# Attention on one Trainium2 core: score banks in fixed groups, wider exponentials, one bank read by two engines, the output product between the value halves

## The chip, the cores and the metric

The kernel runs on one core of one Trainium2 chip. The metric is the device time of one execution, in microseconds (us). A core has five engines with queues of their own: TensorE (PE; its weight loads are listed apart as PEld), VectorE (DVE), ScalarE (ACT), GpSimd (POOL) and SyncE (SP, which issues transfers). They wait for each other through semaphores. Matrix products land in PSUM, which has eight banks of 512 float32 columns in 128 partitions; PSUM is emptied by ScalarE or VectorE.

## The reference

One sequence of S = 2048 tokens with D = 448 features; `x` goes through two branches, mixed by a gate for each token.

```python
g = sigmoid((x * gate_w).sum(-1, keepdims=True))
# attention: 16 heads of 28 features, one shared key and value head
q = (x @ wq) in 16 heads;  k = x @ wk;  v = x @ wv
a = (softmax(q k^T * 28 ** -0.5) v, heads side by side) @ wo
# mixer: shifted tokens, then an MLP, both after a layernorm
x1 = x + shift(gelu(layernorm(x) @ w1)) @ w2
b = x1 + gelu(layernorm(x1) @ w3) @ w4
out = g * a + (1 - g) * b
```

## The kernel before, in words

The program has three stages: projections and token mixing, the MLP, and from about 395 us on the attention, the only stage that the change touches. The instruction order of every engine is the order in which the code issues them.

The attention works in units. A unit `u` is one block of 512 queries and one group of four heads (4 blocks x 4 groups, `NU` = 16 units). A unit has 16 key tiles of 128 keys, taken two at a time, so it has `NV` = 8 steps `v`; the loop over `k` (L1020) runs through 127 steps, and the last one is written out behind it as the tail (L1056 to L1136). One step does this:

- **Scores** (`scores`, L953): for a key tile, four heads side by side, each into a PSUM bank of its own with keys in the partitions and 512 queries in the columns. Three products a head (high and low parts, L958), the four heads of one product issued together: a *score group*. Two key tiles make six groups.
- **Exponentials** (`exps`, L975): ScalarE reads three of the four banks, 512 columns each, and writes exponentials `p` (L985). The fourth bank, head 3 (`DRAIN`), is copied unchanged to SBUF by VectorE (`pd`, L982). When both key tiles are done, ScalarE takes the exponential of both copies in place, 1024 columns in one instruction (`late_exps`, L990).
- **Output product** (`wo_half`, L881): a quarter-sized piece of the product with `wo` for an earlier unit, four 32-partition strips of 224 columns (L859), added to the output by VectorE (`by_one`, L853). Early steps have a piece of the MLP's last product instead (`w4_job`, `w4_half`); the last unit's steps 4 to 6 have two pieces.
- **Values** (`values`, L1002): for the step before, the exponentials times the values and a column of ones (L995), in two halves of 256 queries (`HALVES`). A half sums both key tiles in one bank; VectorE adds it to the unit's running sum `o` (L999) or, in a unit's first step, copies it (L1010). In the profile the float32 product shows as two instructions, so a half is four *value groups* of four.
- Once a unit, its sums are read back, inverted and multiplied in (`sums_begin`, `recip`, `norm`).

What sets the order around the change: PSUM banks are a list. `take()` takes the bank at its front; whoever issues the instruction that empties a bank puts it back at the end. So which banks a step uses moves on from step to step, and each instruction waits for what used its bank last. Exponentials go to a ring of `PB` = 18 tiles, copies to a ring of `PD` = 3.

Of the kernel before, what the change touches and what calls it, by code (L numbers as in the profile page):

```python
# [31 lines left out]
PB = 18  # L32
# [10 lines left out]
def gated_mix_kernel(  # L43
# [16 lines left out]
    psA = ctx.enter_context(tc.tile_pool(name="psA", bufs=1, space=PSUM))  # L60
# [722 lines left out]


    with tc.tile_pool(name="s3", bufs=1, reuse_waits="tile") as s3, \
# [4 lines left out]
        banks = [mm_tile("bank_0"), mm_tile("bank_1"), misc_tile("bank_2"), max_tile("bank_7")]  # L790
        banks += [ps3.tile([P, 512], F32, name=f"bank_{i}") for i in range(3, 7)]
# [70 lines left out]
        def wo_end(u, t, ps, evict=by_one, queue=nc.sync, cols=slice(0, D)):  # L862
# [4 lines left out]
            banks.append(ps)  # L867
# [5 lines left out]
        def wo_job(u, t, cols=slice(0, D), evict=by_one, queue=nc.sync):  # L873
            b, g = divmod(u, NG)
            ps = take()
# [3 lines left out]
            return wo_end(u, t, ps, evict, queue, cols)  # L879

        def wo_half(u, i):  # L881
            t, h = divmod(i, 2)
            wo_job(u, t, slice(224 * h, 224 * h + 224))

        def w4_job(t):
# [3 lines left out]
            ps = bank(f"job_{n}")[:, 0:D]  # L889
# [5 lines left out]
        def w4_half(k, i):  # L895
# [3 lines left out]
            ps = take()  # L899
# [5 lines left out]
            banks.append(ps)  # L905
# [47 lines left out]
        def scores(u, kt):  # L953
            bs = [take() for j in range(4)]
# [5 lines left out]

        p_free = [s3.tile([P, 512], F32, name=f"p_{i}") for i in range(PB)]
        pd_free = [s3.tile([P, 2, 512], F32, name=f"pd_{i}") for i in range(PD)]
# [12 lines left out]
        def exps(u, kt, bs):  # L975
            ps = p_of[u, kt] = {}
            for j in READ:
                if j == DRAIN:
                    if kt % 2 == 0:
                        pd_of[u, kt // 2] = turn_of(pd_free)  # L980
                    ps[j] = pd_of[u, kt // 2][:, kt % 2, :]
                    nc.vector.tensor_copy(ps[j], bs[j])  # L982
                else:
                    ps[j] = turn_of(p_free)
                    behind[kt % 2] = nc.scalar.activation(ps[j], bs[j], AF.Exp, scale=SCALE)  # L985
                banks.append(bs[j])
# [6 lines left out]
        def value(u, kt, q, pv, start, stop):  # L993
            for j in range(4):
                nc.tensor.matmul(pv[32 * j:32 * j + 32, q], vext[:, kt, :], p_of[u, kt][j][:, q],  # L995
                                 start=start, stop=stop, tile_position=(0, 32 * j))

        def add_value(u, q, pv):
            nc.vector.tensor_add(o_of[u][:, q], o_of[u][:, q], pv[:, q])  # L999
            banks.append(pv)  # L1000

        def values(u, v):  # L1002
            if v == 0:
                o_of[u] = s3.tile([P, 512], F32, tag="o", bufs=2, name=f"o_{u}")
            for q in HALVES:
                pv = take()
                for kt in (2 * v, 2 * v + 1):
                    value(u, kt, q, pv, kt % 2 == 0, kt % 2 == 1)
                if v == 0:
                    nc.vector.tensor_copy(o_of[u][:, q], pv[:, q])  # L1010
                    banks.append(pv)
                else:
                    add_value(u, q, pv)
# [3 lines left out]
        READ = (0, 3, 1, 2)  # L1017
        DRAIN = 3

        for k in range(NU * NV - 1):  # L1020
# [7 lines left out]
            for kt in (2 * v, 2 * v + 1):  # L1028
                exps(u, kt, scores(u, kt))
            late_exps(u, v)  # L1030
            if k == 0:
                for t in range(3):
                    w4_job(t)
            if k in (2, 3):
                w4_half(1, k + 4)
            if 4 <= k < 12:
                w4_half(0, k - 4)
            if k == 11:
                weigh_x1(NT - 4, NT)
            if v >= 4 and u:  # L1040
                wo_half(u - 1, v - 4)
            if v < 4 and u > 1:
                wo_half(u - 2, v + 4)
            if v >= 4 and u == NU - 1:
                wo_half(u - 1, v)
# [35 lines left out]
        p14 = p_of[u, NT - 2] = {j: turn_of(p_free) for j in range(DRAIN)}  # L1081
        p14[DRAIN] = turn_of(pd_free)[:, 0, :]
        p15 = p_of[u, NT - 1] = {j: turn_of(p_free) for j in range(4)}
        nc.vector.tensor_copy(p14[DRAIN], b14[DRAIN])
        nc.scalar.activation(p14[0], b14[0], AF.Exp, scale=SCALE)
        for q in HALVES:
            for p, ps in [(p14[1], b14[1]), (p14[2], b14[2]), (p14[DRAIN], p14[DRAIN])] + [(p15[j], b15[j]) for j in READ]:
# [5 lines left out]
        value(u, NT - 4, q0, pvs[0], True, False)  # L1093
        value(u, NT - 3, q0, pvs[0], False, False)
        value(u, NT - 4, q1, pvs[1], True, False)
        value(u, NT - 2, q0, pvs[0], False, False)
        value(u, NT - 1, q0, pvs[0], False, True)
        banks.extend((b14[1], b14[2]))
        add_value(u, q0, pvs[0])
        value(u, NT - 3, q1, pvs[1], False, False)  # L1100
        value(u, NT - 2, q1, pvs[1], False, False)
# [6 lines left out]
        with tc.block():  # L1108
            tc.mark_branch_hint_location("redo", "LikelyTaken", [mybir.EngineType.PE])
            value(u, NT - 1, q1, pvs[1], False, True)  # L1110
        banks.extend(b15)
        add_value(u, q1, pvs[1])
        tail_back(blocks[1])
# [7 lines left out]
        wo_end(u, 1, joint[1])  # L1121
        nc.sync.dma_start(*store0)
# [11 lines left out]
        wo_end(u, 3, joint[3], by_one, nc.scalar)  # L1134
        again = nc.values_load(redo, min_val=0, max_val=P,
# [61 lines left out]
```

## Time and profile before

| What | us |
|---|---|
| median of 3 runs (lowest to highest) | 908.76 (908.12 to 908.85) |
| the profiled execution's own time | 907.61 |
| its span, first to last instruction | 905.8 |
| busy PE / ACT / DVE / POOL in the span | 899.7 / 632.9 / 543.4 / 105.8 |
| late exponentials (L990): count, first and last start | 127, 398.4 and 890.5 |

Times in the profile count from the span's start. A row of a timeline gives start, duration, engine, line, operation, output and inputs; rows of instructions that follow each other are merged, with the count behind the x. Square brackets hold the idle time ahead of an instruction and the instruction that ended it. Recorded durations of one engine may overlap, so its pace is read from start to start.

### The profile page before, as it was taken

Reading aid. Unit: us, or ns where it says so; the run is one execution under the profiler, and the core shown is the slowest. Engines: PE = TensorE matmul, PEld = TensorE weight load, DVE = VectorE, ACT = ScalarE, POOL = GpSimd, SP = SyncE. Lnnn points to the kernel's source line nnn. Section 1 sums busy time; section 2 is a strip of 40 time slices with the busy share of each in tenths; the row PEclk is TensorE's granted clock in tenths of the full one; section 3 lists DMA queues with packets and bytes.
Section 4 is the critical chain, followed back from the end, with each engine's and each line's share of the span. In section 5 each row is a group of like instructions: output and inputs, shape, how many; then the busy total and the mean of one; then the engine's idle time right before and its main releaser. Section 6 shows DMA issues by size and latency. Waiting matters only on the chain.

```text
span 905.8 us, 24129 instructions
## 1 busy us (share of the span) xinstructions
PE 899.7 (99%) x10097; PEld 644.9 (71%) x10097; DVE 543.4 (60%) x1085; ACT 632.9 (70%) x1135; POOL 105.8 (12%) x138
## 2 busy tenths in 40 slices
PE   9999999999999999999999999999999999999997
PEld 7899888888888888875565655655556556565564
DVE  4655364531435646456666676676667766666665
ACT  5443254332131222269999999999999999999995
POOL 3134100221000520011200000000000000000000
PEclk9999999999999999999999999999999999999999
DMA  8876852310312232120000001000011000010001
GB/s 301 318 169 154 231 177 88 72 40 17 64 48 55 45 87 63 27 65 13 26 27 3 26 26 48 22 26 26 7 43 46 26 3 26 19 53 13 15 14 44
DMA packets 50368, 58.23 MB, mean 64 GB/s; under 512 B 9376, under 2 KB 34768, under 8 KB 50256
## 3 DMA queue, kind: packets, MB, share of 16 engines
q1 hardware_dynamic: 47088, 50.95, 20.1%
q10 hardware_dynamic: 3168, 5.70, 1.8%
q8 instruction: 80, 1.31, 0.6%
q14 instruction: 32, 0.26, 0.1%
HBM read 39.80 MB, written 15.59 MB: 61 GB/s over the span
## 4 chain that ended last, share of the span: by engine, by line
PE 99%; ACT 0%; DVE 0%; issue 0%; ACTq 0%; DVEq 0%
PE bank L995 24%; PE bank L958 23%; PE bank L859 8%; PE acc L709 5%; PE acc L708 5%; PE acc L710 5%; PE g L132 4%; PE g L131 4%; PE g L133 4%; PE hs L477 1%; PE hs L478 1%; PE g L134 1%; PE g L135 1%; PE hs L480 1%; PE h L429 1%; PE h L427 1%
## 5 line engine op out<-in xcount | busy, mean ns | idle before, releaser
L985 ACT ACTIVATE p<-bank 128x512 f32<-128x512 f32 x762 | 386.9, 617 | 2.1 <-PE bank L958 2.0
L995 PE MATMUL bank<-p,vext 128*32 128x256 f32 x3076 | 244.4, 379 | 0.0
L995 PE MATMUL bank<-pd,vext 128*32 128x256 f32 x1020 | 241.1, 379 | 0.0
L982 DVE COPY pd<-bank 128x512 f32<-128x512 f32 x254 | 175.3, 691 | 50.6 <-PE bank L958 49.2
L995 PEld LDWEIGHTS bank<-p,vext 128*32 128x32 f32 x3076 | 126.4, 110 | 82.1 <-ACT p L985 0.5
L697 ACT ACTIVATE gh<-g 128x512 fp32r<-128x512 f32 x54 | 32.2, 597 | 182.0 <-PE g L135 182.0
L999 DVE TENSOR_TENSOR o<-o,bank 128x256 f32<-128x256 f32 x222 | 93.5, 421 | 92.5 <-ACT p L985 54.1
L990 ACT ACTIVATE pd<-pd 128x1024 f32<-128x1024 f32 x127 | 141.0, 1110 | 0.0
L958 PE MATMUL bank<-qh,kH 30*128 30x512 f32 x1024 | 117.9, 444 | 0.0
L995 PEld LDWEIGHTS bank<-pd,vext 128*32 128x32 f32 x1020 | 111.9, 110 | 0.1
L700 DVE TENSOR_TENSOR gl<-gf,gh 128x512 fp32r<-128x512 f32 x54 | 37.2, 688 | 117.7 <-ACT gf L698 117.6
L958 PE MATMUL bank<-qh,kL 28*128 28x512 f32 x1024 | 105.0, 392 | 0.0
L958 PE MATMUL bank<-ql,kH 28*128 28x512 f32 x1024 | 105.0, 391 | 0.0
L958 PEld LDWEIGHTS bank<-qh,kH 30*128 30x128 f32 x1024 | 60.7, 182 | 58.0 <-ACT p L985 46.0
L709 PE MATMUL acc<-w4l,gh 128*128 128x448 f32 x216 | 78.9, 365 | 0.0
L708 PE MATMUL acc<-w4h,gh 128*128 128x448 f32 x216 | 78.8, 365 | 0.0
L710 PE MATMUL acc<-w4h,gl 128*128 128x448 f32 x216 | 78.7, 364 | 0.0
L859 PE MATMUL bank<-wof,on 128*32 128x224 f32 x1008 | 73.1, 367 | 0.0
L132 PE MATMUL g<-al,w3h 128*128 128x512 f32 x168 | 65.8, 392 | 0.0
L131 PE MATMUL g<-ah,w3h 128*128 128x512 f32 x168 | 65.6, 390 | 0.0
L133 PE MATMUL g<-ah,w3l 128*128 128x512 f32 x168 | 65.5, 390 | 0.0
L958 PEld LDWEIGHTS bank<-ql,kH 28*128 28x128 f32 x1024 | 51.6, 185 | 9.2
(203 smaller groups left out, 1158.8 us busy)
## 6 DMA issues: line engine op xcount, KB each, us to landing
qd<-qf ACTq DMA_DIRECT2D x16, 256.0 KB
qm<-qd SPq DMA_DIRECT2D x16, 256.0 KB
qr<-qd SPq DMA_DIRECT2D x16, 256.0 KB
rb<-rd SPq DMA_DIRECT2D x15, 256.0 KB
x<-in_x_dram SPq DMA_DIRECT2D x4, 896.0 KB
hd<-ht SPq DMA_DIRECT2D x16, 224.0 KB
hr<-hd SPq DMA_DIRECT2D x8, 448.0 KB
w34raw<-in_w_dram SPq DMA_DIRECT2D x7, 512.0 KB
```

Of the source, the lines that this page charges most:

```text
L131: nc.tensor.matmul(ps, wh[:, c, :], ah[:, c, :], start=(c == 0), stop=False)
L132: nc.tensor.matmul(ps, wh[:, c, :], al[:, c, :], start=False, stop=False)
L133: nc.tensor.matmul(ps, wl[:, c, :], ah[:, c, :], start=False, stop=False)
L708: nc.tensor.matmul(ps, gh[:, tok], w4h[i][:, k, :], start=(f == 0), stop=False)
L709: nc.tensor.matmul(ps, gh[:, tok], w4l[i][:, k, :], start=False, stop=False)
L710: nc.tensor.matmul(ps, gl[:, tok], w4h[i][:, k, :], start=False, stop=(f == stop))
L859: nc.tensor.matmul(ps[32 * j:32 * j + 32, cols], on_of[u][:, tok], wof[:, u % NG, cols], start=start, stop=stop, tile_position=(0, 32 * j))
L958: nc.tensor.matmul(bs[j], w, a, start=(i == 0), stop=(i == 2), tile_position=(32 * j, 0))
L982: nc.vector.tensor_copy(ps[j], bs[j])
L985: behind[kt % 2] = nc.scalar.activation(ps[j], bs[j], AF.Exp, scale=SCALE)
L990: ins = nc.scalar.activation(pd, pd, AF.Exp, scale=SCALE)
L995: nc.tensor.matmul(pv[32 * j:32 * j + 32, q], vext[:, kt, :], p_of[u, kt][j][:, q], start=start, stop=stop, tile_position=(0, 32 * j))
```

## The change

PSUM in the attention stage is no longer a list of eight single banks. The pool of the earlier stages (`psA`) is closed first, and five fixed tiles are made: for even key tiles `even_0` (one bank), `even_12` (two) and `even_3` (one), for odd key tiles `odd_012` (three) and `odd_3` (one). Scores of head j go to bank j of their group.

ScalarE empties `even_0` and `even_12` with one instruction each (512 and 1024 columns) and `odd_012` with one of 1536. `even_3` is split: VectorE copies columns 256 to 511 and ScalarE takes the exponential of columns 0 to 255. `odd_3` is copied whole by VectorE. The copies, 256 and 512 columns, lie side by side in one tile of 768, and the late exponential covers these. A step so has five exponentials over the same 4096 columns in place of seven.

The value halves have fixed banks: half 0 goes to `even_3`, half 1 to `odd_3` (`single`). `values` is called once for each half; half 0 comes right behind the scores, then the output product (in `even_0`), the sums' check and the norm where due, then half 1. The tail is adapted in names only; it keeps its order. The diff, cut:

```diff
-        banks = [mm_tile("bank_0"), mm_tile("bank_1"), misc_tile("bank_2"), max_tile("bank_7")]
-        banks += [ps3.tile([P, 512], F32, name=f"bank_{i}") for i in range(3, 7)]
+        even = [ps3.tile([P, 512], F32, name="even_0"), ps3.tile([P, 2, 512], F32, name="even_12"),
+                ps3.tile([P, 512], F32, name="even_3")]
+        odd = [ps3.tile([P, 3, 512], F32, name="odd_012"), ps3.tile([P, 512], F32, name="odd_3")]
+        heads = [[even[0], even[1][:, 0, :], even[1][:, 1, :], even[2]],
+                 [odd[0][:, j, :] for j in range(3)] + [odd[1]]]
+        single = [even[2], odd[1]]
+        banks = []
...
         def scores(u, kt):
-            bs = [take() for j in range(4)]
+            bs = heads[kt % 2]
...
-        def exps(u, kt, bs):
-            ps = p_of[u, kt] = {}
-            for j in READ:
-                if j == DRAIN:
-                    if kt % 2 == 0:
-                        pd_of[u, kt // 2] = turn_of(pd_free)
-                    ps[j] = pd_of[u, kt // 2][:, kt % 2, :]
-                    nc.vector.tensor_copy(ps[j], bs[j])
-                else:
-                    ps[j] = turn_of(p_free)
-                    behind[kt % 2] = nc.scalar.activation(ps[j], bs[j], AF.Exp, scale=SCALE)
-                banks.append(bs[j])
+        def exps(u, v):
+            pd = pd_of[u, v] = turn_of(pd_free)
+            pe, po = turn_of(pe_free), turn_of(po_free)
+            scores(u, 2 * v)
+            nc.vector.tensor_copy(pd[:, 0:256], even[2][:, HALVES[1]])
+            nc.scalar.activation(pe[:, 1536:1792], even[2][:, HALVES[0]], AF.Exp, scale=SCALE)
+            nc.scalar.activation(pe[:, 0:512], even[0], AF.Exp, scale=SCALE)
+            behind[0] = nc.scalar.activation(pe[:, 512:1536], even[1].rearrange("p j q -> p (j q)"), AF.Exp, scale=SCALE)
...
+            scores(u, 2 * v + 1)
+            nc.vector.tensor_copy(pd[:, 256:768], odd[1])
+            nc.scalar.activation(po, odd[0], AF.Exp, scale=SCALE)
...
-            for kt in (2 * v, 2 * v + 1):
-                exps(u, kt, scores(u, kt))
+            exps(u, v)
             late_exps(u, v)
...
+            else:
+                values(*divmod(k - 1, NV), 0)
...
             if v >= 4 and u:
-                wo_half(u - 1, v - 4)
+                wo_half(u - 1, v - 4, even[0])
...
-            if k:
-                values(*divmod(k - 1, NV))
-            if u and v == 0:
-                sums.append(sums_begin(u - 1, o_of[u - 1]))
             if u and v == 1:
                 norms.append(recip(*sums.pop()))
             if u and v == 3:
                 norm(*norms.pop())
+            if k:
+                values(*divmod(k - 1, NV), 1)
+            if u and v == 0:
+                sums.append(sums_begin(u - 1, o_of[u - 1]))
```

How the built program stands, at three places. The number behind a tile's name is the build's own; brackets name the semaphores that an instruction waits for, by the engine that raises them. First ScalarE, one step of unit 13, before (banks `bank_*`, exponentials `p_*`, copies `pd_*`):

```order
L985 ACTIVATE p_6_3504<-bank_6_3491 128x512 [waits PE_49]
L985 ACTIVATE p_7_3505<-bank_1_3485 128x512 [waits PE_49]
L985 ACTIVATE p_8_3506<-bank_0_3484 128x512 [waits PE_49]
L985 ACTIVATE p_9_3507<-bank_7_3487 128x512 [waits PE_49]
L985 ACTIVATE p_10_3508<-bank_4_3489 128x512 [waits DVE_49,PE_49]
L985 ACTIVATE p_11_3509<-bank_3_3488 128x512 [waits DVE_49,PE_49]
L990 ACTIVATE pd_1_3517<-pd_1_3517 128x1024 [waits DVE_49,Activation_49]
```

and now (the first row is the late exponential of the step before; `pe_*` and `po_*` hold the exponentials of even and odd key tiles):

```order
L1009 ACTIVATE pd_2_3504<-pd_2_3504 128x768 [waits DVE_49,Activation_49]
L998 ACTIVATE pe_0_3496<-even_3_3487 128x256 [waits DVE_49]
L999 ACTIVATE pe_0_3496<-even_0_3485 128x512
L1000 ACTIVATE pe_0_3496<-even_12_3486 128x1024
L1004 ACTIVATE po_0_3499<-odd_012_3488 128x1536 [waits PE_49]
```

Seven rows became five; the one that reads `even_3` stands first and waits for VectorE, and those of `even_0` and `even_12` behind it have no wait of their own. Then VectorE, one step of unit 13, before:

```order
L982 COPY pd_2_3518<-bank_4_3489 128x512 [waits PE_49]
L982 COPY pd_2_3518<-bank_1_3485 128x512 [waits PE_49]
L853 SCALAR_TENSOR_TENSOR ot_13_9978<-bank_0_3484,gg_75,x1_72 128x224 [waits PE_49,DMAHW7_49,Activation_49,Pool_49]
L999 TENSOR_TENSOR o_13_9683<-o_13_9683,bank_4_3489 128x256 [waits DVE_49,PE_49]
L999 TENSOR_TENSOR o_13_9683<-o_13_9683,bank_7_3487 128x256 [waits DVE_49,PE_49,Activation_49]
```

and now:

```order
L997 COPY pd_1_3503<-even_3_3487 128x256 [waits PE_49]
L1003 COPY pd_1_3503<-odd_3_3489 128x512 [waits PE_49]
L1018 TENSOR_TENSOR o_13_9451<-o_13_9451,even_3_3487 128x256 [waits PE_49,Activation_49]
L859 SCALAR_TENSOR_TENSOR ot_12_9638<-even_0_3485,gg_75,x1_72 128x224 [waits PE_49,Activation_49]
L1018 TENSOR_TENSOR o_13_9451<-o_13_9451,odd_3_3489 128x256 [waits DVE_49,PE_49]
```

The first copy is half as wide, and the output product's eviction (L853, now L859) moved from ahead of both value additions to between them. Last TensorE, from the output product into the values in unit 14, before:

```order
L859 MATMUL bank_2_3486<-wof_3482,on_6_7014 32x224 [waits Activation_49]
L859 MATMUL bank_2_3486<-wof_3482,on_6_7014 32x224 x3
L995 MATMUL bank_6_3491<-p_12_3510,vext_73 32x256 [waits DVE_49]
L995 MATMUL bank_6_3491<-p_13_3511,vext_73 32x256
L995 MATMUL bank_6_3491<-p_14_3512,vext_73 32x256
L995 MATMUL bank_6_3491<-pd_2_3518,vext_73 32x256
```

and now, from the last odd scores to the next even scores:

```order
L966 MATMUL odd_3_3489<-ql_6_5634,kH_1020 128x512
L1014 MATMUL even_3_3487<-pe_2_3498,vext_73 32x256 [waits Activation_49]
L1014 MATMUL even_3_3487<-pe_2_3498,vext_73 32x256 x3
L1014 MATMUL even_3_3487<-po_2_3501,vext_73 32x256 x3
L1014 MATMUL even_3_3487<-pd_2_3504,vext_73 32x256
L865 MATMUL even_0_3485<-wof_3483,on_5_6421 32x224 [waits Activation_49]
L865 MATMUL even_0_3485<-wof_3483,on_5_6421 32x224 x3
L1014 MATMUL odd_3_3489<-pe_2_3498,vext_73 32x256 [waits DVE_49]
L1014 MATMUL odd_3_3489<-pe_2_3498,vext_73 32x256 x2
L1014 MATMUL odd_3_3489<-pd_2_3504,vext_73 32x256
L1014 MATMUL odd_3_3489<-po_2_3501,vext_73 32x256 x3
L1014 MATMUL odd_3_3489<-pd_2_3504,vext_73 32x256
```

The first value half now stands ahead of the product and waits for ScalarE; the product waits for ScalarE's reading of `even_0`, and the second half for VectorE's copy of `odd_3`.

More of the change, by code (lines that the diff above doesn't have):

```diff
@@ L871, in wo_end, with wo_job @@
             return store
-        def wo_job(u, t, cols=slice(0, D), evict=by_one, queue=nc.sync):
+        def wo_job(u, t, cols=slice(0, D), evict=by_one, queue=nc.sync, ps=None):
             b, g = divmod(u, NG)
-            ps = take()
+            own = ps is None
+            if own:
+                ps = take()
             wo_part(u, t, cols, ps, True, True)
@@ L878, in wo_job, with wo_half, w4_job @@
                 ot_of[4 * b + t] = s3.tile([P, D], F32, tag="ot", bufs=5, name=f"ot_{4 * b + t}")
-            return wo_end(u, t, ps, evict, queue, cols)
-        def wo_half(u, i):
+            store = wo_end(u, t, ps, evict, queue, cols)
+            if own:
+                banks.append(ps)
+            return store
+        def wo_half(u, i, ps):
             t, h = divmod(i, 2)
-            wo_job(u, t, slice(224 * h, 224 * h + 224))
-        def w4_job(t):
+            wo_job(u, t, slice(224 * h, 224 * h + 224), ps=ps)
+        def w4_job(t, ps):
             n = NT - 4 + t
@@ L1109, in gated_mix_kernel @@
             tc.mark_branch_hint_location("redo", "LikelyTaken", [mybir.EngineType.PE])
[L1110 removed]
+            value(u, NT - 1, 1, pvs[1], False, True)
         banks.extend(b15)
         add_value(u, q1, pvs[1])
+        banks.append(pvs[1])
         tail_back(blocks[1])
@@ L1121, in gated_mix_kernel @@
         wo_end(u, 1, joint[1])
+        banks.append(joint[1])
         nc.sync.dma_start(*store0)
```

90 lines of the change are left out of this document (49 added, 41 removed).

## The prediction

> **What bounds the kernel now.** The page comes first: the share of each engine, its slices, and the chain that ended last.
>
> ```profile
> span 905.8 us, 24129 instructions
> PE 899.7 (99%) x10097; PEld 644.9 (71%) x10097; DVE 543.4 (60%) x1085; ACT 632.9 (70%) x1135; POOL 105.8 (12%) x138
> ...
> ACT  5443254332131222269999999999999999999995
> ...
> PE 99%; ACT 0%; DVE 0%; issue 0%; ACTq 0%; DVEq 0%
> ```
>
> PE is busy in 99% of the span and carries the chain, but ScalarE (ACT) changes in slice 19: from there on, the attention stage, it is full. The change touches only that stage, so it is read apart. The busy time of 100 us in its middle:
>
> ```profile
> core 0: us, PE busy (x) PEld busy (x) DVE busy (x) ACT busy (x) POOL busy (x), PEclk, DMA share, GB/s
> 500.00:600.00 100.00, 100.00 (x1648) 60.26 (x1648) 69.45 (x139) 100.00 (x181) 5.68 (x6) 1.00 0.11 33
> ```
>
> Both PE and ACT read 100, at full granted clock. Matmuls overlap, so a busy PE may still wait; the timeline of one step, engine by engine (ScalarE, TensorE, its weight loads PEld, VectorE), tells which of the two sets the pace. Rows give start, duration, engine and line, in brackets the idle time ahead and who ended it:
>
> ```profile
> 605.08 1.11 ACT L990 ACTIVATE pd<-pd 128x1024 f32<-128x1024 f32 x1
> 606.10 3.04 ACT L985 ACTIVATE p<-bank 128x512 f32<-128x512 f32 x6
> 608.97 1.11 ACT L990 ACTIVATE pd<-pd 128x1024 f32<-128x1024 f32 x1
> ```
> ```profile
> 605.09 0.51 PE L958 MATMUL bank<-qh,kH 30*128 30x512 f32 x4
> 605.43 0.40 PE L958 MATMUL bank<-qh,kL 28*128 28x512 f32 x4
> 605.66 0.40 PE L958 MATMUL bank<-ql,kH 28*128 28x512 f32 x4
> ...
> 606.75 0.58 PE L859 MATMUL bank<-wof,on 128*32 128x224 f32 x8
> 607.15 0.39 PE L995 MATMUL bank<-p,vext 128*32 128x256 f32 x3
> ...
> 607.80 0.39 PE L995 MATMUL bank<-p,vext 128*32 128x256 f32 x3
> ...
> 608.66 0.39 PE L995 MATMUL bank<-p,vext 128*32 128x256 f32 x3
> ```
> ```profile
> 605.09 0.19 PEld L958 LDWEIGHTS bank<-qh,kH 30*128 30x128 f32 x4 [0.41 <-ACT p L985]
> ...
> 606.75 0.16 PEld L859 LDWEIGHTS bank<-wof,on 128*32 128x32 f32 x8 [0.42 <-ACT p L985]
> ```
> ```profile
> 606.20 1.40 DVE L982 COPY pd<-bank 128x512 f32<-128x512 f32 x2 [0.49 <-PE bank L958]
> 607.51 0.44 DVE L853 SCALAR_TENSOR_TENSOR ot<-bank,gg,ot 128x224 f32<-128x224 f32 x1
> 608.26 0.42 DVE L999 TENSOR_TENSOR o<-o,bank 128x256 f32<-128x256 f32 x1 [0.31 <-PE bank L995]
> ```
>
> A step is 608.97 - 605.08 = 3.89 us, and ACT has no idle time in it: one late exponential (1.02 to the next start) and six of 512 columns, (608.97 - 606.10) / 6 = 0.478 each. PE waits for ACT twice (the brackets on PEld). Its own work is six score groups at 0.23 (605.43 to 605.66), one output product at 0.40 (606.75 to 607.15) and eight value groups at (608.66 - 607.15) / 7 = 0.216, 1.38 + 0.40 + 1.73 = 3.51. So ACT sets the pace, with PE 0.38 behind it.
>
> **The change, part by part.** *Fewer, wider exponentials.* Five replace seven over the same 4096 columns. What one instruction costs beside its columns comes from the tail, where exponentials of 256 columns stand back to back:
>
> ```profile
> 892.67 0.39 ACT L1088 ACTIVATE p<-bank 128x256 f32<-128x256 f32 x1
> ...
> 893.24 1.78 ACT L1088 ACTIVATE p<-bank 128x256 f32<-128x256 f32 x6
> 894.82 0.49 ACT L1088 ACTIVATE pd<-pd 128x256 f32<-128x256 f32 x1
> ```
>
> Six starts take 894.82 - 893.24 = 1.58, 0.263 each; 512 columns took 0.478, so 256 columns are 0.215 and the fixed part is 0.05. The new sum, start to start: 0.26 (256) + 0.48 (512) + 0.91 (1024) + 1.34 (1536) + 0.81 (the late one, 768 columns: 1.02 - 0.215) = 3.79. If ACT kept the pace, a step would gain 0.10. No row reads several banks in one instruction. Its bounds are these sums and, if each further bank were charged like an instruction of its own, 0.15 more, 3.94; I take no extra charge, since a column costs the same in all the rows.
>
> The Trainium skill ("ScalarE: Activation LUTs", What ACT_TABLE_LOAD costs) gives an ACTIVATE without pointer operands 186 ns plus 0.833 ns a column, with back-to-back ones overlapping by about 93 ns. By it seven would cost some 4.06 and five 3.88, a gain of 0.19; the measured step of 3.89 is below 4.06, so the row's 0.05 is used.
>
> *The bank that two engines empty.* In the built order L998, ACT's exponential of 256 columns of even_3, waits for VectorE (DVE) alone, no longer for PE. It can learn that the scores are there only from L997, DVE's copy of the other half of that bank, which itself waits for PE. So the two reads stand one behind the other, DVE first. Behind the waiting L998 in ACT's queue are the exponentials of even_0 and even_12, whose banks are ready at the same time, and everything after them. And PE's first value group writes even_3, so it waits for L998.
>
> *The output product between the values, fixed banks.* Before, each score set, product and value half took the banks that were freed longest ago, and the first value half needed none that the step's last scores had just filled. Now PE runs even scores, odd scores, values half 0 (into even_3), product (even_0), values half 1 (odd_3), even scores. The product's 0.40 is moved, not added. This is a loop through three engines, and its length is added up from the start of the even scores. The copy of 256 columns and the hand-overs have these rows:
>
> ```profile
> L1010 DVE COPY o<-bank x32: 423/425/426, 401.3 to 870.5; 128x256 f32<-128x256 f32 x32
> ```
> ```profile
> 377.87 0.59 ACT L698 ACTIVATE gf<-g 128x512 f32<-128x512 f32 x1
> ```
> ```profile
> 378.49 0.69 DVE L700 TENSOR_TENSOR gl<-gf,gh 128x512 fp32r<-128x512 f32 x1 [1.53 <-ACT gf L698]
> ```
> ```profile
> 896.75 0.31 DVE L1077 STREAM_TRANSPOSE on<-scaled 128x128 f32<-128x128 f32 x1
> ```
> ```profile
> 897.11 0.16 PEld L859 LDWEIGHTS bank<-wof,on 128*32 128x32 f32 x8 [0.50 <-DVE on L1077]
> ```
>
> - even scores, first group to third: 2 x 0.23 = 0.46; third group's start to DVE's copy: 606.20 - 605.66 = 0.54 (even_3 is written last in each group, as the copied bank was);
> - copy of 256 columns: 0.43;
> - DVE to ACT: no row shows ACT waiting for DVE; ACT to DVE took 378.49 - (377.87 + 0.59) = 0.03, DVE to PE 897.11 - (896.75 + 0.31) = 0.05, PE to DVE 606.20 - (605.66 + 0.40) = 0.14. I take 0.05, bounds 0.03 and 0.14;
> - exponential of 256 columns to its end: 0.39 (the row at 892.67);
> - ACT to PE: 0.05 again; PE's restart after idling: 0 to 0.11 (the score group at 605.09 was followed after 0.34 instead of 0.23); the product at 606.75, of the values' kind, took 0.20 a group from a standstill, so I take 0.02;
> - values 4 x 0.216 = 0.87, product 0.40, values 0.86.
>
> Sum: 0.46 + 0.54 + 0.43 + 0.05 + 0.39 + 0.05 + 0.02 + 0.87 + 0.40 + 0.86 = 4.07. Of the 1.94 ahead of the values the odd scores cover PE up to 1.38; 0.56 is idle. ACT's 3.79 fits in with 0.28 to spare, so its gain is hidden by this loop.
>
> Other waits in the loop: odd scores need odd_012 read. ACT starts L998 at 1.48 (0.46 + 0.54 + 0.43 + 0.05) and reaches the odd banks 1.65 later, at 3.13; 1.34 and a hand-over later, at some 4.6, they are free, 0.1 ahead of the next odd scores (4.07 + 0.69). Half 1 needs the copy of odd_3, done by 1.15 (the third odd group) + 0.54 + 0.70 (half of 1.40) = 2.4, ahead of its 3.2. PE's next even scores need even_0 evicted: from the start of half 0, its last group at 0.65, 0.46 to DVE's add (607.80 to 608.26), the add 0.42, the eviction 0.44, 0.05, together 2.02, plus a cold restart of 0.11: 2.13, exactly PE's own 2.13. The loop holds with nothing to spare there. SP's DMAs and POOL's splits keep their order and their steps; the sums' readback (15 units) has its reader moved ahead of values half 1, 0.9 us earlier in a step, and is taken as hidden.
>
> **The sum.** The late exponentials count the steps:
>
> ```profile
> L990 ACT ACTIVATE pd<-pd x127: 1104/1107/1247, 398.4 to 890.5; 128x1024 f32<-128x1024 f32 x127
> ```
> ```profile
> 881.98 1.10 ACT L990 ACTIVATE pd<-pd 128x1024 f32<-128x1024 f32 x1
> 883.37 3.05 ACT L985 ACTIVATE p<-bank 128x512 f32<-128x512 f32 x6 [0.29 <-PE bank L958]
> 886.24 1.11 ACT L990 ACTIVATE pd<-pd 128x1024 f32<-128x1024 f32 x1
> ```
>
> 126 steps take 492.1 us. The first two, without the full set of work, I leave at 3.8 (ACT's sum); the last two hold a second product and took 4.26 with ACT waiting for PE, which shows that PE's loop before was 4.26 - 0.40 = 3.86, just under ACT's 3.89. After: 2 x 3.8 + 122 x 4.07 + 2 x 4.47 = 513.1, 21.0 more. The start and the tail keep their instructions and are left at zero; the tail's score and value groups wait for each other as before, and I allow 1 us either way. The profiled execution took 907.61 us (905.8 of span and 1.8 around it), so 928.6; the median of the runs shown, 908.76, is 1.15 above that execution: 930, rounded.
>
> **The rivals.** *ACT keeps the pace (faster).* If the two reads of even_3 ran side by side, the loop would lose the 0.43 and 0.05 (4.07 - 0.48 = 3.59) and ACT's 3.79 would decide: 122 x 0.10 = 12 us less, and 1 to 2 in the last steps, 895. It decides once the loop is under 3.79. For it: the diff reads the two halves in two instructions of two engines. Against it: L998's only wait is on DVE. Chance 0.05, for a wait that I read wrongly.
> The Trainium skill ("PSUM — Partial Sum Buffer", PSUM bank collisions raise a hardware error) says that two engines must not access one bank in the same partitions at once, reads included, and that different columns do not help. By that rule the wait is needed, and this case is not to be had; no run here shows a collision.
>
> *The loop comes out at 3.89 (no change).* It needs 0.18 less: hand-overs of 0.03 and ACT releasing even_3 well before the end of its record. 909 us, chance 0.04.
>
> *DVE's eviction decides (slower still).* The chain from half 0 through add and eviction to the even scores ties with PE's. Every 0.1 by which DVE is later than this is a step of 4.17, 12 us more, 942. For it: DVE also has the norms and the sums' check to do in two of eight steps. Against it: back-to-back DVE records overlap (the eviction begins at 607.51, ahead of the copies' end at 607.60). Chance 0.20.
>
> **The numbers.** The forecast, the loop at 4.0 to 4.13, has 0.71, at 930. One term wrong by 0.1 moves it by 12 us; with its low ends (hand-overs 0.03, no restart: 4.01) it is 922, and 3.97 gives 918; with the eviction late 944. Range 917 to 944, leaving out the two first rivals and the far end of the third. A measurement of this kernel tells 0.2% (1.8 us) from no change: faster 0.05, same 0.04, slower 0.91.
>
> **What would show it.** Right: L1009 every 4.07 us; ACT idle some 0.28 ahead of L998, ended by DVE's L997; PE's weight load of L1014 idle some 0.5 ahead of half 0, ended by ACT's L998; ACT busy 93% of the stage. L1000 and L1004 with 0.91 and 1.34 to the next start would confirm the price of width. Wrong: ACT without idle time and L1009 under 3.89 apart; or L998 starting together with L997.

## The result, and the profile after

The changed kernel takes 945.18 us (median of 4 runs, 943.91 to 946.03), the kernel before 908.49: a ratio of 1.040, 95% interval 1.0385 to 1.0421. It is slower by 36.7 us where 21 were forecast, and it ends 1.2 us above the range. The side and the mechanism are those of the forecast, the step is longer than it said.

The page of the changed kernel, the lines that stand against those of before:

```profile
span 942.1 us, 23614 instructions
...
PE 903.8 (96%) x10097; PEld 644.6 (68%) x10097; DVE 516.7 (55%) x1085; ACT 627.8 (67%) x881; POOL 105.5 (11%) x138
...
ACT  5442355321221221399999999999999999999985
...
PE 85%; DVE 7%; ACT 6%; issue 1%; DMA 0%; DVEq 0%; ACTq 0%
```

The chain no longer runs through PE alone: VectorE has 7% of it and ScalarE 6%. The same 100 us of the attention stage as before:

```profile
500.00:600.00 100.00, 94.32 (x1540) 56.03 (x1540) 58.94 (x130) 92.53 (x121) 5.69 (x6) 1.00 0.10 28
```

Both engines that read 100 now have gaps, ScalarE 7.5%, PE 5.7%, and the clock is still 1.00. The groups of the page say where (mean ns of one, then the idle time ahead and who ended it):

```profile
L997 DVE COPY pd<-even 128x256 f32<-128x256 f32 x127 | 53.9, 424 | 56.9 <-PE even L966 56.9
...
L1014 PEld LDWEIGHTS even<-pe,vext 128*32 128x32 f32 x1034 | 20.8, 108 | 85.1 <-ACT pe L998 84.2
...
L998 ACT ACTIVATE pe<-even 128x256 f32<-128x256 f32 x127 | 48.6, 383 | 39.8 <-DVE pd L997 39.7
```

Read from below: ScalarE waits 39.7 us for VectorE's copy of half of even_3, the weight loads of value half 0 wait 84.2 us for ScalarE's half, and VectorE waits for PE's even scores. The timeline of one step shows this loop closing, ScalarE, then TensorE, its weight loads and VectorE:

```profile
602.93 1.47 ACT L1004 ACTIVATE po<-odd 128x1536 f32<-128x1536 f32 x1
604.26 0.87 ACT L1009 ACTIVATE pd<-pd 128x768 f32<-128x768 f32 x1
605.43 0.38 ACT L998 ACTIVATE pe<-even 128x256 f32<-128x256 f32 x1 [0.30 <-DVE pd L997]
605.71 0.59 ACT L999 ACTIVATE pe<-even 128x512 f32<-128x512 f32 x1
606.18 1.03 ACT L1000 ACTIVATE pe<-even 128x1024 f32<-128x1024 f32 x1
607.09 1.48 ACT L1004 ACTIVATE po<-odd 128x1536 f32<-128x1536 f32 x1
```
```profile
603.95 0.51 PE L966 MATMUL even<-qh,kH 30*128 30x512 f32 x4
604.28 0.40 PE L966 MATMUL even<-qh,kL 28*128 28x512 f32 x4
604.52 0.40 PE L966 MATMUL even<-ql,kH 28*128 28x512 f32 x4
...
605.87 0.64 PE L1014 MATMUL even<-pe,vext 128*32 128x256 f32 x8 [0.24 <-ACT pe L998]
...
606.54 0.39 PE L1014 MATMUL even<-po,vext 128*32 128x256 f32 x3
...
606.75 0.56 PE L865 MATMUL even<-wof,on 128*32 128x224 f32 x8
607.13 0.39 PE L1014 MATMUL odd<-pe,vext 128*32 128x256 f32 x3
...
607.78 0.39 PE L1014 MATMUL odd<-po,vext 128*32 128x256 f32 x3
...
608.11 0.51 PE L966 MATMUL even<-qh,kH 30*128 30x512 f32 x4
```
```profile
605.86 0.16 PEld L1014 LDWEIGHTS even<-pe,vext 128*32 128x32 f32 x8 [0.68 <-ACT pe L998]
...
606.94 0.12 PEld L1014 LDWEIGHTS odd<-pe,vext 128*32 128x32 f32 x3
...
608.11 0.19 PEld L966 LDWEIGHTS even<-qh,kH 30*128 30x128 f32 x4 [0.41 <-DVE ot L859]
```
```profile
604.97 0.42 DVE L997 COPY pd<-even 128x256 f32<-128x256 f32 x1 [0.46 <-PE even L966]
...
607.44 0.45 DVE L859 SCALAR_TENSOR_TENSOR ot<-even,gg,x 128x224 f32<-128x224 f32 x1
```

A step is 608.11 - 603.95 = 4.16 us. In order: even scores to their third group 0.57, to the copy 0.45, copy to ScalarE 0.46, ScalarE to half 0 0.44, half 0 0.88, product 0.38, half 1 to the next even scores 0.98. The forecast's loop is there piece for piece. Two of its pieces are longer than was put in: the first score group takes 0.33 to the second (0.23 had been put in for each), and the last value group 0.33 to the even scores (0.216 had been put in). One is shorter: the third score group takes 0.45 to the copy (0.54 had been put in).

The whole difference between the two profiled executions, 943.91 - 907.61 = 36.3 us, divides by the late exponentials:

```profile
L1009 ACT ACTIVATE pd<-pd x127: 865/867/872, 400.5 to 926.3; 128x768 f32<-128x768 f32 x127
```

The 126 steps take 525.8 us (before 492.1): 33.7 more. The first late exponential starts 2.1 us later (400.5, before 398.4), and what follows the last one is about half a microsecond longer (942.1 - 926.3 = 15.8, before 905.8 - 890.5 = 15.3).

### The profile page after: what moved, and what is told of

It reads as the page before. It is cut to its first block, busy times and chain, and to the rows that moved or that the text cites. A ratio compares the mean times of both kernels' runs of the same rounds, so it can differ in the third digit from the quotient of the medians.

```text
span 942.1 us, 23614 instructions
## 1 busy us (share of the span) xinstructions
PE 903.8 (96%) x10097; PEld 644.6 (68%) x10097; DVE 516.7 (55%) x1085; ACT 627.8 (67%) x881; POOL 105.5 (11%) x138
## 4 chain that ended last, share of the span: by engine, by line
PE 85%; DVE 7%; ACT 6%; issue 1%; DMA 0%; DVEq 0%; ACTq 0%
PE even L1014 15%; PE even L966 12%; PE odd L1014 11%; DVE pd L997 6%; ACT pe L998 5%; PE even L865 5%; PE acc L710 5%; PE acc L709 5%; PE acc L711 5%; PE g L133 4%; PE g L132 4%; PE g L134 4%; PE hs L478 1%; PE hs L479 1%; PE g L135 1%
## 5 line engine op out<-in xcount | busy, mean ns | idle before, releaser
L1004 ACT ACTIVATE po<-odd 128x1536 f32<-128x1536 f32 x127 | 187.1, 1473 | 0.0
L1000 ACT ACTIVATE pe<-even 128x1024 f32<-128x1024 f32 x127 | 131.1, 1033 | 0.0
L1014 PE MATMUL odd<-pd,vext 128*32 128x256 f32 x504 | 129.3, 379 | 0.0
L1014 PE MATMUL even<-pe,vext 128*32 128x256 f32 x1034 | 83.0, 391 | 29.3 <-ACT pe L998 29.2
L1009 ACT ACTIVATE pd<-pd 128x768 f32<-128x768 f32 x127 | 110.2, 867 | 0.0
L1003 DVE COPY pd<-odd 128x512 f32<-128x512 f32 x127 | 87.8, 692 | 39.0 <-PE odd L966 39.0
L1014 PE MATMUL even<-po,vext 128*32 128x256 f32 x784 | 79.6, 379 | 0.0
L1014 PEld LDWEIGHTS even<-pe,vext 128*32 128x32 f32 x1034 | 20.8, 108 | 85.1 <-ACT pe L998 84.2
L1014 PE MATMUL even<-pd,vext 128*32 128x256 f32 x262 | 77.4, 379 | 0.0
L1014 PE MATMUL odd<-pe,vext 128*32 128x256 f32 x756 | 76.6, 379 | 0.0
L1014 PE MATMUL odd<-po,vext 128*32 128x256 f32 x756 | 76.6, 379 | 0.0
L999 ACT ACTIVATE pe<-even 128x512 f32<-128x512 f32 x127 | 75.2, 592 | 0.0
L998 ACT ACTIVATE pe<-even 128x256 f32<-128x256 f32 x127 | 48.6, 383 | 39.8 <-DVE pd L997 39.7
```

The costliest lines, as they stand in the source:

```text
L998: nc.scalar.activation(pe[:, 1536:1792], even[2][:, HALVES[0]], AF.Exp, scale=SCALE)
L1000: behind[0] = nc.scalar.activation(pe[:, 512:1536], even[1].rearrange("p j q -> p (j q)"), AF.Exp, scale=SCALE)
L1004: nc.scalar.activation(po, odd[0], AF.Exp, scale=SCALE)
L1009: ins = nc.scalar.activation(pd, pd, AF.Exp, scale=SCALE)
L1014: nc.tensor.matmul(pv[32 * j:32 * j + 32, HALVES[i]], vext[:, kt, :], p_of[u, kt][j][i], start=start, stop=stop, tile_position=(0, 32 * j))
```

## The experiments

**Theory A**: the step is the length of one loop (even scores, emptying of the bank that half 0 takes, half 0, product, half 1, even scores). **Rival B**: ScalarE sets the pace, because its whole queue stands behind VectorE's copy. **Rival C**: VectorE's eviction of the product holds the even scores back; the prediction priced that case at 4.17 us a step and 942 us, nearly what was measured, and the row of L966 above names L859 as the releaser. **Rivals D and E**: that two engines share a bank, or that the product stands between the values, is the cost as such. The kernel before took 908.0 to 908.1 us beside all of these. The steps given below are medians over a run, from one late exponential's start to the next; ratios are to the kernel before, with their 95% interval.

### ScalarE first, VectorE second

```diff
-            nc.vector.tensor_copy(pd[:, 0:256], even[2][:, HALVES[1]])
             nc.scalar.activation(pe[:, 1536:1792], even[2][:, HALVES[0]], AF.Exp, scale=SCALE)
+            nc.vector.tensor_copy(pd[:, 0:256], even[2][:, HALVES[1]])
```

> ScalarE reads its half of even_3 first, VectorE copies the other half second; nothing else differs. Theory A (a loop PE -> emptying of even_3 -> values -> product -> values -> even scores sets the step): the two reads still stand one behind the other, so the step stays at 4.16 us (4.1 to 4.2) and the time at 943 to 946 us (up to 2 us less if the start loses its wait for VectorE); the weight load of half 0 is then released by VectorE's copy. Rival B (the step is long because ScalarE's whole queue stands behind VectorE's copy): ScalarE no longer waits for VectorE, so the step falls towards its own sum, 3.80, and the time to some 900 us.

Measured: 943.65 us, ratio 1.039 (1.0373 to 1.0408). The waits of its attention stage, 500 to 800 us (us in total, times, longest):

```profile
PEld even L1014 <- DVE pd L998: 48.6, 72, 0.7
...
ACT pe L997 <- PE even L966: 22.1, 72, 0.3
```

ScalarE now waits for PE and never for VectorE, and the step is still 4.167. B falls: it does not matter which engine reads first, only that the bank is released after both.

### VectorE alone empties even_3

```diff
...
-            nc.vector.tensor_copy(pd[:, 0:256], even[2][:, HALVES[1]])
-            nc.scalar.activation(pe[:, 1536:1792], even[2][:, HALVES[0]], AF.Exp, scale=SCALE)
+            nc.vector.tensor_copy(pd[:, 0:512], even[2])
...
-            nc.vector.tensor_copy(pd[:, 256:768], odd[1])
+            nc.vector.tensor_copy(pd[:, 512:1024], odd[1])
...
```

> VectorE alone copies all 512 columns of even_3 (0.69 us, as its copy of odd_3 takes), ScalarE has four exponentials, the late one of 1024 columns (its own sum 0.48 + 0.90 + 1.33 + 1.02 = 3.73). Theory A: in the loop 0.425 + 0.033 + 0.383 become 0.69: 0.15 less, step 4.01, 124 steps x 0.15 = 19 us less, 926 us. Rival B (ScalarE's wait for VectorE sets the step): ScalarE has no wait behind a copy any more, step 3.75 to 3.85, 895 to 906 us. Rival C (VectorE is the bound through its eviction): more copying on VectorE, no gain or a loss, 945 us or more.

Measured: 930.30 us, ratio 1.0248 (1.0231 to 1.0265), step 4.067. One engine alone, with a longer copy, is 15 us faster than two in turn; A has the direction, and 0.06 of the step is left over. One step, VectorE and PE:

```profile
607.89 0.69 DVE L997 COPY pd<-even 128x512 f32<-128x512 f32 x1 [0.36 <-PE even L966]
```
```profile
607.38 0.41 PE L966 MATMUL even<-ql,kH 28*128 28x512 f32 x4
```

The copy starts 607.89 - 607.38 = 0.51 after the third score group, where the copy of 256 columns started 0.45 after it (0.54 in the kernel before, also for 512). This is the 0.06; why the wider copy starts later is open.

### The eviction does not read the product

```diff
+        def unread(n, ps, before, cols):
+            nc.vector.scalar_tensor_tensor(ot_of[n][:, cols], x1[:, n, cols], gg[:, n:n + 1], before,
+                                           op0=ALU.mult, op1=ALU.add)
...
-            wo_job(u, t, slice(224 * h, 224 * h + 224), ps=ps)
+            wo_job(u, t, slice(224 * h, 224 * h + 224), evict=unread, ps=ps)
```

> The eviction of the output product (L859 in the attention stage) reads a block of x1 from SBUF instead of the product in PSUM: same engine, same size, but PE's next even scores no longer wait for it; the product is computed and left unread, so the output lacks it. Theory A (the 0.33 of the last value group is a cost of TensorE's turn from values to scores, as before): step stays at 4.16, 943 to 946 us. Rival C (the eviction through VectorE holds the even scores back): the last value group takes 0.22 and the first score group 0.23 to 0.34, step 3.94 to 4.05, 917 to 931 us.

Measured: 944.31 us, ratio 1.0397 (1.038 to 1.0415), step 4.163. Waits of its stage, and the turn in one step, TensorE:

```profile
PEld even L970 <- issue: 29.6, 72, 0.4
```
```profile
606.03 0.39 PE L1018 MATMUL odd<-po,vext 128*32 128x256 f32 x3
...
606.36 0.51 PE L970 MATMUL even<-qh,kH 30*128 30x512 f32 x4
606.70 0.40 PE L970 MATMUL even<-qh,kL 28*128 28x512 f32 x4
606.93 0.41 PE L970 MATMUL even<-ql,kH 28*128 28x512 f32 x4
```

Nothing waits for an eviction any more, and the same 0.41 us ahead of the even scores' weight load is now put down to "issue", which means that the profile shows nothing the engine waited for. The spacings are the same 0.33, 0.34, 0.23. C falls, though its number was met. The kernel before has these spacings too (last value group, even scores):

```profile
608.66 0.39 PE L995 MATMUL bank<-p,vext 128*32 128x256 f32 x3
...
608.99 0.51 PE L958 MATMUL bank<-qh,kH 30*128 30x512 f32 x4
609.32 0.41 PE L958 MATMUL bank<-qh,kL 28*128 28x512 f32 x4
```

There its PE rows were not what set the step, so nobody paid for them.

### An added turn from values to scores

Two score matmuls of head 0 are added between half 0 and the product, into even_0, which the product then overwrites.

```diff
+            for i in range(2):
+                for _, _, w, a in score(u, even[0], 0, slice(0, P), i=i):
+                    nc.tensor.matmul(even[0], w, a, start=(i == 0), stop=(i == 1), tile_position=(0, 0))
             if k in (2, 3):
                 w4_half(1, k + 4, even[0])
```

> The changed kernel with two more score matmuls (head 0, into even_0, overwritten by the product) between value half 0 and the product of each step: one more turn of TensorE from values to scores, with nothing to wait for. If the turn itself costs 0.11 us ahead of the first score group and 0.11 ahead of the second, a step grows by 2 x 0.23 + 0.22 = 0.68 us, 126 x 0.68 = 86 us, to 1031 us, and the first of them starts some 0.33 after the last value group. If the turn is free and the even scores wait for something else, a step grows by 0.46 us, to 1003 us, with spacings of 0.22 and 0.23.

Measured: 1045.79 us, ratio 1.1515 (1.1498 to 1.1533), step 4.959, 0.80 more. The weight load of the added scores waits for no other engine (500 to 800 us), and TensorE in one step:

```profile
PEld even L1052 <- issue: 24.7, 60, 0.4
```
```profile
608.42 0.39 PE L1014 MATMUL even<-po,vext 128*32 128x256 f32 x3
...
608.75 0.50 PE L1052 MATMUL even<-qh,kH 30*128 30x512 f32 x1
609.09 0.40 PE L1052 MATMUL even<-qh,kL 28*128 28x512 f32 x1
609.41 0.59 PE L865 MATMUL even<-wof,on 128*32 128x224 f32 x8
```

0.33, 0.34, and then 0.32 to the product, in place of the 0.21 from half 0 to the product (606.54 to 606.75 in the changed kernel's step): 0.78 in all. The turn towards scores costs the 0.11 twice, in a place where the step did not turn before. The time is still 15 us above the 1031 expected. What none of the theories had is the way back, 0.32 instead of 0.23, another 0.09; with it the step grows by 0.78, and that is the measured growth but for 0.02.

### One more exponential on ScalarE

An exponential of 256 columns from SBUF to an unused tile is added behind the late one.

```diff
...
             late_exps(u, v)
+            nc.scalar.activation(extra, wof[:, 0, 0:256], AF.Exp, scale=SCALE)
```

> One more exponential of 256 columns (SBUF to an unused tile) on ScalarE in each step, behind the late one: 0.26 to 0.28 us more work for ScalarE. Theory A: ScalarE has 0.3 us idle ahead of its part of even_3, so the extra work fills it: no change, 943 to 948 us, ScalarE idle 0.1 or less. Rival B (ScalarE sets the pace): 127 x 0.27 = 34 us more, 979 us.

Measured: 945.06 us, ratio 1.0407 (1.039 to 1.0425). The groups of ScalarE in its stage, the last two:

```profile
L1046 ACT ACTIVATE extra<-wof 128x256 f32<-128x256 f32 x72 | 31.5, 438 | 0.0
L999 ACT ACTIVATE pe<-even 128x256 f32<-128x256 f32 x72 | 27.7, 384 | 0.5 <-DVE pd L998 0.4
```

The idle time ahead of even_3's exponential is gone, from 22 us in this stretch to 0.5, and the time is not changed. ScalarE's saving by wider exponentials was worth nothing here.

### Another bank for half 0, and one engine for even_3

The first kernel exchanges two banks and the order of two exponentials; the second lets ScalarE alone empty even_3, first in its queue.

```diff
-        single = [even[2], odd[1]]
+        single = [even[0], odd[1]]
...
             nc.vector.tensor_copy(pd[:, 0:256], even[2][:, HALVES[1]])
+            nc.scalar.activation(pe[:, 0:512], even[0], AF.Exp, scale=SCALE)
             nc.scalar.activation(pe[:, 1536:1792], even[2][:, HALVES[0]], AF.Exp, scale=SCALE)
-            nc.scalar.activation(pe[:, 0:512], even[0], AF.Exp, scale=SCALE)
...
-                wo_half(u - 1, v - 4, even[0])
+                wo_half(u - 1, v - 4, even[2])
...
```

> Values half 0 go into even_0, the product into even_3 (the two banks exchanged), and ScalarE reads even_0 first, its half of even_3 second; all work is the same and even_3 is still read by both engines. Theory A (the loop through the bank that half 0 takes): even_0 is emptied by one exponential of 512 columns, 0.60 instead of 0.425 + 0.033 + 0.383 = 0.84, so the step falls by 0.24 to 3.92 and the time to some 915 us (910 to 922). Rival D (the cost is that two engines share a bank, wherever it stands): no change, 945 us. Rival E (the product between the values costs): no change, 945 us.

```diff
...
-            nc.vector.tensor_copy(pd[:, 0:256], even[2][:, HALVES[1]])
-            nc.scalar.activation(pe[:, 1536:1792], even[2][:, HALVES[0]], AF.Exp, scale=SCALE)
+            nc.scalar.activation(pe[:, 1536:2048], even[2], AF.Exp, scale=SCALE)
...
```

> ScalarE alone empties even_3, with one exponential of 512 columns first in its queue; VectorE copies only odd_3, the late exponential has 512 columns (ScalarE's sum 0.48 + 0.48 + 0.90 + 1.33 + 0.59 = 3.78). Theory A: the loop has 0.60 in place of 0.84: step 3.92, 915 us (910 to 922), as in the run before. Rival E (the product's place between the values): 945 us. If VectorE being spared a copy mattered beside this, the time would come out under the run before.

Measured: 909.86 us, ratio 1.0022 (1.0013 to 1.0032), and 913.52 us, ratio 1.0062 (1.0045 to 1.0078); steps 3.892 and 3.919. In the first, even_3 is still read by both engines one after the other, the product still stands between the values, and 35 of the 37 us are gone: D and E fall. The second has the step that A forecast, 3.92; the first comes out just under its range of 910 to 922 us. Rows of the first, ScalarE and the weight loads of TensorE:

```profile
603.41 0.86 ACT L1009 ACTIVATE pd<-pd 128x768 f32<-128x768 f32 x1
604.30 0.60 ACT L998 ACTIVATE pe<-even 128x512 f32<-128x512 f32 x1
604.81 0.38 ACT L999 ACTIVATE pe<-even 128x256 f32<-128x256 f32 x1
```
```profile
604.95 0.15 PEld L1014 LDWEIGHTS even<-pe,vext 128*32 128x32 f32 x7 [0.41 <-ACT pe L998]
```

The weight load of half 0 still has ScalarE as its releaser, but after 0.41 instead of 0.68; in the run with the added turn the product's weight load stood idle for 0.36 to 0.37 after scores with nothing to wait for, so little of the 0.41 is ScalarE's. The late exponential is followed after 0.89, where the forecast's sum had 0.81, so ScalarE has at most 0.08 left. TensorE's own work in a step, the prediction's 3.51 with the turn there and back (0.11, 0.11 and 0.09), is some 3.82, an estimate from the spacings above. So the loop, ScalarE and TensorE are nearly level here.

### The product ahead of both halves

```diff
-            else:
-                values(*divmod(k - 1, NV), 0)
             if k in (2, 3):
...
             if k:
+                values(*divmod(k - 1, NV), 0)
                 values(*divmod(k - 1, NV), 1)
```

> The product is put back ahead of both value halves, as before the change; banks, widths and readers as in the changed kernel. Theory A: the product then waits for even_0's exponential, which comes after that of even_3: odd scores' cover of PE is the same, but the wait grows by 0.28 + 0.48 + 0.05 - 0.05 = about 0.75 ahead of the product, less 0.38 of it that no longer stands between the halves but ahead of them: nothing is covered in exchange, so the loop is 0.58 + 0.45 + 0.43 + 0.03 + 0.28 + 0.60 + 0.05 + 0.38 + 0.87 + 0.98 = 4.65, 61 us more, about 1005 us. Rival E (the product between the values is what costs time): faster than the changed kernel, 909 to 930 us.

Measured: 1006.74 us, ratio 1.1092 (1.1073 to 1.111), step 4.650, as A's sum has it. One weight load shows why:

```profile
607.03 0.16 PEld L865 LDWEIGHTS even<-wof,on 128*32 128x32 f32 x8 [1.17 <-ACT pe L999]
```

The order of before, in these banks, waits 1.17 us for even_0. Moving the product behind half 0 saved 62 us of what the fixed banks would have cost.

### Values two steps behind

A new order, in outline: values of two steps ago, half 0 and the product both in odd_3, half 1 in even_3.

```diff
...
+            exps_even(u, v)
+            if k:
+                late_exps(*divmod(k - 1, NV))
...
+                w = divmod(k - 2, NV)
+                values(*w, 0, odd[1])
...
+            ps = odd[1][:, 256:480]
...
+                ends.append(wo_half(u - 1, v - 4, ps))
...
+                values(*w, 1, even[2])
...
+            exps_odd(u, v)
...
```

> A version built on theory A so that no value half waits for a bank that the same step's scores have just filled: order on PE even scores, values half 0 (of two steps ago, into odd_3), product (into free columns of odd_3), values half 1 (into even_3, emptied by VectorE alone), odd scores; ScalarE has 512, 1024, late 1024 and 1536 columns; the table of the exponential is loaded ahead of the first scores. All work is kept. Theory A: no loop is left that is longer than PE's own work, 6 x 0.235 + 0.39 + 8 x 0.216 + 0.22 for one turn from values to scores = 3.75, or ScalarE's 3.73 to 3.8: step 3.75 to 3.85, 893 to 905 us, faster than before the change. Rival (the banks odd_3 and even_3, now emptied three times in a step by VectorE, form a loop through VectorE): step 3.9 or more, 909 us or more.

Measured: 958.67 us, ratio 1.0551 (1.0533 to 1.0568): a failure, and slower than the changed kernel. Its waits, 500 to 800 us:

```profile
PEld odd L1034 <- DVE pd L1023: 36.6, 70, 0.7
...
PEld odd L897 <- DVE on L848: 15.7, 9, 2.2
DVE on L848 <- DMA rb<-rd: 14.8, 9, 2.1
```

The odd scores now stand right ahead of the next even scores, so half 0 waits for VectorE's copy of the odd_3 that was just filled. The expectation had looked only at the scores of the same step; the loop had moved across the step's end, and by A's own way of adding up (odd scores 0.57, to the copy 0.55, copy and hand-over 0.74, half 0 0.89, product 0.38, half 1 0.97) it is 4.10, the median step measured. That alone is under the changed kernel's 4.163; the waits above point to the norm for the rest: with one step less for its readback, VectorE waits for the DMA (14.8 us in 9 units), and the product for VectorE. No run takes this part out.

### The start

```diff
+        loaded = s3.tile([P, 1], F32, name="loaded")
+        nc.scalar.activation(loaded, ones1, AF.Exp)
```

> The changed kernel with the same early exponential of one column, nothing else. The first late exponential started 2.1 us later than before the change; if that is the table's load standing behind the wait for VectorE's first copy (copy's end 396.13, load 396.22 to 397.51), it goes by 1.3 us: 943.9 us. Otherwise no change, 945.2 us.

> The kernel with even_0 for half 0 and even_3 for the product (the run that took 909.9 us), and one exponential of a single column on a constant ahead of the first scores, so that the table of the exponential is loaded before the scores are there. Theory A with the start counted apart: the load of 1.28 us no longer stands behind VectorE's or PE's wait, 1.3 us less, 908.6 us, within 0.2% of the kernel before. Rival (the start's 2 us lie elsewhere): 909.9 us.

Measured, with the changed kernel: 944.16 us, ratio 1.0395 (1.0381 to 1.0409), which the interval does not tell from the changed kernel. The traces tell more. ScalarE at the start of the stage, changed kernel, then with the early load:

```profile
396.22 1.28 ACT L998 ACT_TABLE_LOAD   x1 [3.00 <-DVE pd L997]
397.52 0.38 ACT L998 ACTIVATE pe<-even 128x256 f32<-128x256 f32 x1
```
```profile
394.01 1.28 ACT L982 ACT_TABLE_LOAD   x1
...
396.98 0.38 ACT L1000 ACTIVATE pe<-even 128x256 f32<-128x256 f32 x1 [1.05 <-DVE pd L999]
```

In the changed kernel the load waits for VectorE's copy although it needs nothing of it, and the first exponential starts 1.4 us after the copy's end (396.13); with the early load it is 0.1 (396.89). In this execution the stages before ended later (VectorE's last row of additions there, L781, began at 393.51, in the changed kernel at 392.75), so the first late exponential starts only 0.5 earlier, at 399.97. In the kernel before, the load stood at 393.30 and waited for nothing. With the banks exchanged as well: 908.04 us, ratio 1.0 (0.9991 to 1.0009), against 1.0022 (1.0013 to 1.0032) without it. Those two intervals are apart, by 1.8 us. This is the best version found, and it only equals the kernel before; none that beats it was found.

## Why the prediction was wrong in size

- *The loop sets the step, not ScalarE.* Right. Swapping the readers, adding work to ScalarE and taking the eviction out of it changed nothing; a shorter emptying of half 0's bank gave 0.27 us of the step back, and a longer way to the product cost 0.49.
- *Wider exponentials.* Right: L998 to L999, to L1000, to L1004 0.28, 0.47 and 0.91, and L1009 follows L1004 after 604.26 - 602.93 = 1.33, so several banks in one instruction cost nothing extra. ScalarE's idle time was 0.30 (0.28 forecast), its busy share 92.5% (93%).
- *Copy, exponential, hand-overs.* Copy 0.42, exponential 0.38, ScalarE to PE 0.05: right. PE to copy 0.45 instead of 0.54, 0.09 too much, which was taken from a copy of 512 columns.
- *"even scores, first group to third: 2 x 0.23 = 0.46" and "values ... 0.86"*: these are the steps that failed, 0.11 and 0.12 short. The prediction saw the 0.34 at 605.09, took it for "PE's restart after idling", put in 0.02 for a restart at half 0 and, in its sum, nothing at the even scores. It comes with the turn from values to scores, which every step makes once, whether TensorE had to wait or not. The Trainium skill ("TensorEngine Tiling (Array Packing)", Tiling Modes, Key Properties) says that changing the tiling mode, and not just the tile, drains TensorE; values and scores have different modes, the runs agree, and the prediction had not weighed that rule. With both, 4.07 + 0.23 - 0.09 = 4.21; the small rest (restart, product, hand-overs, rounding) brings it to the 4.16 measured. On 122 steps 0.09 is 11 us.
- *"3.51 ... PE 0.38 behind"*: too low by the same turns; with them TensorE's own work is some 3.82, as estimated above. The prediction could have met this: from the last two steps it read 3.86 for PE's loop, 0.35 more than its own sum, and did not ask why.
- *Steps at the ends.* The first two took 4.17 and 3.79 (3.8 each forecast), the last two 4.72 and 4.71 (4.47): 0.9 us.
- *"The start ... left at zero"*: 2.1 us, of which 1.4 are the table's load behind VectorE's copy; the rest goes with the copy itself, which starts at 395.71 right behind an older operation in VectorE's queue. The tail: 0.5, inside its 1.
- *The rivals.* "DVE's eviction decides" had 942 us and the nearest number; the run without a read of the product shows that it was not the cause, so its near hit was luck. (The range's upper end of 944 names that case too and has no sum of its own.) A releaser that the profile names is the last event ahead of the instruction, not always what it waited for: L859's record ended at 607.89, and the load came at 608.11.

With turn and start in their places, 122 x 0.09 + 0.9 + 2.1 + 0.5 = 14.5 on top of 928.6 gives 943.1, beside 943.91 in the profiled execution.

## What to carry to other kernels

When fixed buffers replace a rotation, write down for each buffer what it waits for, and add up the longest closed way through the engines; here the time followed that way and not the engine that was busiest before. Measure the spacing of instructions where their kind changes, not only within a run of equal ones: a cost that another engine hid before becomes part of the loop. And where two engines must empty one buffer in turn, give that buffer to work that comes later, here the product instead of half 0.

## What the runs showed of the hardware

- TensorE pays for turning between two kinds of tiles. From value groups (128 rows, 32 columns a tile) to score groups (28 or 30 rows, 128 columns) the first group comes 0.33 us after the last instead of 0.216, and the second 0.34 after the first instead of 0.23, with nothing to wait for; the way back was 0.32 in place of 0.23 where it was not hidden. Not all of this needs a turn: at the start of the stage in the changed kernel the weight load of the odd scores, behind even scores, was held for 0.24 us (395.24, put down to VectorE), and there too the second group came late, 0.31 after the first (395.27 and 395.58). The operands differ in type as well, declared float32 for the values and float32r for the scores in the code; no run separates type from shape, though the first scores of the stage, behind float32r groups of 128 rows and 128 columns, also came 0.30 after the last (394.16 and 394.46) where these groups follow each other after 0.20. The weight load of the first score group starts together with its matmuls (both 608.11), while a value group's load starts 0.19 ahead of its matmuls (606.94 and 607.13).
- One exponential over two or three banks costs by its columns alone: 1024 columns 0.91, 1536 columns 1.33 to the next start. The fixed 0.05 of each is near the 51 ns that the Trainium skill ("Perfetto Trace Analysis", Optimizing Scalar/DVE Operations) gives for ScalarE on PSUM.
- A table load on ScalarE can take over the waits of the instruction that needs it: here 1.28 us behind a copy that it did not need, where the kernel before had it ahead of the wait.
